# Sliding-window attention and a multiplicative FFN on one core: batch 0's Q and K in thirds, w1 and w2 in column quarters, and a new order of the first phase

## The chip, the core and the metric

The kernel runs on one core of a Trainium2 chip. The metric is the device time of one execution in microseconds (us), median of several runs. Engines are named as in the profile: PE (TensorE, matrix multiplies), PEld (its weight loads), DVE (VectorE), ACT (ScalarE), POOL (GpSimd) and SP (SyncE). Each engine works through its own list of instructions in the order in which the program lists them. POOL also issues the transfers that cast from 32-bit to 16-bit floats on their way into the chip; an instruction that issues a transfer stands in POOL's list like any other.

## What is computed

For 8 batches, 8 heads, 576 tokens and a head width of 64, with q, k and v in 32-bit floats:

```
scores = q @ k.T / 8, kept where 0 <= query - key < 64
attn   = softmax(scores);  x = attn @ v, put together as [4608 tokens, 512]
out    = ((x @ w1) * (x @ w2)) @ w3 @ w_out        w1, w2: [512, 1024]; w3: [1024, 1024]; w_out: [1024, 512]
```

## The kernel before, in words

**Fold.** Since nothing stands between w3 and w_out, the kernel computes `wc = w3 @ w_out` once, in eight blocks of 128 rows. `fold_t(fc)` (line 469) transposes one block of w3 by eight 128-wide multiplies with the identity (line 474) and copies it out of PSUM (476); `fold_mm(fc, c0, c1, cp)` (478) multiplies it with columns c0 to c1 of w_out (481) and copies the result out (482). Four transposed blocks fit at a time.

**Attention.** `load_qk(b, which)` (202) brings Q or K of a batch in by four POOL transfers, one for each pair of heads, into 32 partitions each. In batches 0 to 2 a partition takes runs of 9 tokens (line 200). `transposes(b, which, hh)` (219) turns a half of the heads over on DVE (225). `scores(n)` (272) multiplies for a third of a batch (192 queries, all 8 heads; line 286) into two PSUM tiles `a_ps`; `weigh(d)` (296) takes the exponential of one of these tiles on ACT (303) and cuts the window out, with a multiply by a ready band on DVE (308), or with two or four selects on POOL (258, 260). `values(d)` (314) multiplies with V (337 in the first three batches) and, with the sums of the same multiplication, normalises: a logarithm and an exponential on ACT (343, 344), a multiply on DVE into `xT` (345). There are two `a_ps` buffers in all, for scores and values together. `load_v` (232) brings blocks of 128 tokens of V, `copy_v` (240) copies the overlap of two blocks on DVE; the columns of ones beside V are set once (512). `keep_sums` stores the logarithms for a check at the end.

**FFN.** `ffn_ab(g, fc, nf, lo, hi)` (401) computes `(x @ w1) * (x @ w2)` for a group of 512 tokens or a half of it: matmuls into two of the four `f_ps` buffers (417), a copy of the first on ACT (422), the product on DVE (423). `ffn_o(g, t)` (426) multiplies 128 tokens with `wc` (435), copies (437) and stores through SP (444).

**Order.** The schedule is written out by hand. Lines 516 to 620 are the first phase: the loads of batch 0 and of the weights, the fold, batch 0 and 1 of attention, FFN group 0 and a part of group 1. In it `keep_busy(n)` (502) puts n multiplies of the identity with itself on PE. `make_identity` is two POOL instructions, `make_bands` (265) eight. From `tick(24)` at line 614 on, a loop places attention steps (`tick`) between FFN steps; that loop is the same before and after.

Of the kernel before, what the change touches and what calls it, by code (L numbers as in the profile page):

```python
# [8 lines left out]
FP32 = mybir.dt.float32  # L9
FP16 = mybir.dt.float16  # L10
# [134 lines left out]
def kernel(  # L145
# [22 lines left out]
    NU = 12 * B  # L168
    NS = 3 * B
    SHORT = 3  # L170
    EARLY = 2

    keep = ctx.enter_context(tc.tile_pool(name="keep", bufs=1))
    ident16 = keep.tile([P, P], FP16)
# [22 lines left out]

    t16s, kTs, qTs = {}, {}, {}

    RUN = [9] * 3 + [2] * (B - 3)  # L200

    def load_qk(b, which, *hhs):
        src = k if which == "k" else q
        r = RUN[b]
        if (which, b) not in t16s:
            t16s[which, b] = sb.tile([P, 2, TI * D], FP16, name=which + "16", bufs=2)
        t = t16s[which, b]
        if not hhs:
            for j in range(NJ):
                nc.gpsimd.dma_start(  # L210
                    out=t[32 * j:32 * j + 32].rearrange("p hh (i n) -> p (hh i) n", n=r * D),
                    in_=src[b, 2 * j:2 * j + 2].rearrange("hh (i p r) d -> p (hh i) (r d)", p=32, r=r))
        for hh in hhs:
            for i in range(2):
                nc.gpsimd.dma_start(
                    out=t[:, hh, i * r * D:(i + 1) * r * D],
                    in_=src[b, hh:H:2, i * 32 * r:(i + 1) * 32 * r].rearrange("j (p r) d -> j p (r d)", p=32, r=r))

    def transposes(b, which, hh):

        dst = kTs if which == "k" else qTs
        r = RUN[b]
        if hh == 0:
            dst[b] = sb.tile([P, 2, S, 2], FP16, name=which + "T")
        nc.vector.transpose(  # L225
            dst[b][:, hh].rearrange("q t c -> q (t c)").bitcast(I32).rearrange("q (i p r) -> q i r p", p=32, r=r),
            t16s[which, b][:, hh].bitcast(I32).rearrange("p (i r e) -> p i r e", r=r, e=32))

    def v_heads(b):
        return v16s[b % 2].rearrange("p c j (a e) -> p c (j a) e", a=2)[:, :, :, 0:D]  # L230
# [38 lines left out]

    held = {}  # L270

    def scores(n, now=True):

        b, si = divmod(n, 3)
        kT, qT = kTs[b], qTs[b]
        seg = SEGS[si]
        w = sum(blk[2] for blk in seg)
        s_ps = [ps_a.tile([P, 2, 512], FP32, name="a_ps") for _ in range(2)]
        c0 = 0
        for (k0, q0, m, _) in seg:  # L280
            for a in range(2):
                for c in range(2):
                    for j in range(NJ):
                        part = slice(32 * j, 32 * j + 32)
                        o0 = 256 * a + c0
                        nc.tensor.matmul(s_ps[j // 2][:, j % 2, o0:o0 + m], kT[part, a, k0:k0 + P, c],  # L286
                                         qT[part, a, q0:q0 + m, c], start=(c == 0), stop=(c == 1),
                                         skip_group_check=True)
# [3 lines left out]
        weigh(2 * n)  # L292
        if now:
            weigh(2 * n + 1)

    def weigh(d):

        s_ps = held.pop(d)
        si = d // 2 % 3
        w = s_ps.shape[-1]  # L300

        pt = sb.tile([P, 2, 2, 256], FP16, name="pt", bufs=6)
        nc.scalar.activation(pt[:, :, :, 0:w], s_ps, AF.Exp, bias=-SHIFT, scale=scale)  # L303

        rows = pt.rearrange("k j a n -> k (j a) n")
        if d % 2 == 1 and d < 6 * EARLY:
            band = bands[min(si, 1)]
            nc.vector.tensor_tensor(rows[:, :, 0:w], rows[:, :, 0:w],  # L308
                                    band[:, 0:w].unsqueeze(1).broadcast_to([P, 4, w]), ALU.mult)
        else:  # L310
            select(rows, si)
        probs[d] = pt

    def values(d):
# [4 lines left out]
        pt = probs.pop(d)  # L319
        seg = SEGS[si]  # L320
        q_base = seg[0][1]
        o_ps = ps_a.tile([P, 2, 512], FP32, name="a_ps")
        if jp == 0:
            lns[b, si] = sb.tile([P, NJ, 192], FP32, name="ln_s", bufs=4)
        y = lns[b, si][:, j0:j0 + 2]
        r = sb.tile([P, 2, 192], FP32, name="r")
        x0 = (b * S + q_base) % RING
        xs = xT[:, j0:j0 + 2, x0:x0 + 192]
        if b < SHORT:

            for jj in range(2):
                c0 = 0
                for bi, (k0, q0, n, _) in enumerate(seg):
# [8 lines left out]
            o, total = (o_ps[:, e, 0:384].rearrange("p (j n) -> p j n", j=2) for e in range(2))  # L342
            nc.scalar.activation(y, total, AF.Ln)
            nc.scalar.activation(r, y, AF.Exp, scale=-1.0)  # L344
            nc.vector.tensor_tensor(xs, o, r, ALU.mult)  # L345
            return
        for jj in range(2):
            first = True
            for a in range(2):
                c0 = 0  # L350
                for bi, (k0, q0, n, _) in enumerate(seg):
# [4 lines left out]
                                     start=first, stop=(bi == 1), skip_group_check=True)  # L356
                    first = False
                    c0 += n
        nc.scalar.activation(y[0:D], o_ps[D:P, :, 0:192], AF.Ln)  # L359
        nc.scalar.activation(y[D:P], o_ps[0:D, :, 192:384], AF.Ln)  # L360
        nc.scalar.activation(r, y, AF.Exp, scale=-1.0)  # L361
# [21 lines left out]
    def tick(u):  # L383

        b, r = divmod(u, 12)
        n, m = divmod(u, 4)
        if m == 0 and n < NS:
            scores(n, now=False)
        if m == 1 and n < NS:
            weigh(2 * n + 1)  # L390
        if m in (1, 2) and 6 < n <= NS:
            values(2 * n - 3 + m)
        for e in late.get(r, []):
            event(b, *e)
        if m == 3 and 6 < n <= NS:
            keep_sums(n - 1)
# [54 lines left out]
        return w3a[:, 2 * fc:2 * fc + 2, :] if fc < 4 else \  # L451
            xT[:, fc - 4, 2 * S:2 * S + DF].rearrange("p (a n) -> p a n", a=2)

    def load_w12(i, half):
        cols = slice(half * 512, half * 512 + 512)
        nc.gpsimd.dma_start(out=(w1_sb, w2_sb)[i][:, :, cols],
                            in_=(moe_w1, moe_w2)[i][:, cols].rearrange("(c p) n -> p c n", p=P))

    def load_wo(half):
        cols = slice(half * 256, half * 256 + 256)  # L460
        nc.gpsimd.dma_start(out=wo16[:, :, cols], in_=moe_w_out[:, cols].rearrange("(e p) m -> p e m", p=P))  # L461

    def load_w3(n):
        fc = 2 * n
        dst = w3a[:, 2 * fc:2 * fc + 4, :].rearrange("p (f a) n -> p f (a n)", f=2) if n < 2 else \
            xT[:, fc - 4:fc - 2, 2 * S:2 * S + DF]
        nc.gpsimd.dma_start(out=dst, in_=moe_w3[fc * P:fc * P + 2 * P].rearrange("(f p) n -> p f n", p=P))

    def fold_t(fc):

        w3 = w3_rows(fc).rearrange("p a (e n) -> p (a e) n", n=P)
        tp = ps_f.tile([P, 8, P], FP16, name="f_ps")
        for ec in range(8):
            nc.tensor.transpose(tp[:, ec, :], w3[:, ec, :], ident16)  # L474
# [38 lines left out]

    w3Ts = {}

    load_qk(0, "k")
    make_identity(nc, ident16)
    load_qk(0, "q")
    load_wo(0)
    load_w3(0)  # L520
    make_bands()
    load_w3(1)
    load_wo(1)
    load_w3(2)
    load_v(0, 0, 2, 3)
    for i in range(2):
        ones_of(i, nc.vector)
    for which in "kq":
        for hh in range(2):
            transposes(0, which, hh)  # L530
    keep_busy(120)
    scores(0)
    keep_busy(30)
    fold_t(0)
    fold_t(1)
    scores(1)
    load_w3(3)
    load_v(0, 4, 5)
    fold_mm(0, 0, 256, act_cp)
    fold_mm(1, 0, 256, act_cp)  # L540
    fold_t(2)
    fold_t(3)
    scores(2)
    for i in range(2):
        load_w12(i, 0)
    fold_mm(2, 0, 256, act_cp)
    fold_mm(3, 0, 256, act_cp)
    fold_mm(0, 256, DM, act_cp)
    fold_mm(1, 256, DM, act_cp)
    fold_t(4)  # L550
    fold_t(5)
    fold_mm(2, 256, DM, act_cp)
    fold_mm(3, 256, DM, act_cp)
    copy_v(0, 1)
    fold_mm(4, 0, DM, act_cp)
    values(0)
    values(1)
    fold_t(6)
    fold_mm(5, 0, DM, act_cp)
    values(2)  # L560
    values(3)
    copy_v(0, 4)
    fold_t(7)
    fold_mm(6, 0, DM, act_cp)
    values(4)
    values(5)
    fold_mm(7, 0, DM, act_cp)
    for i in range(2):
        load_w12(i, 1)
    load_qk(1, "k")  # L570
    load_qk(1, "q")
    load_v(1, 0, 2, 3, 4, 5)
    for n in range(3):
        keep_sums(n)
    for fc in range(8):
        ffn_ab(0, fc)
        if 2 <= fc < 6:
            transposes(1, "kkqq"[fc - 2], fc % 2)
    load_qk(2, "k")
    load_qk(2, "q")  # L580
    copy_v(1, 1)
    copy_v(1, 4)
    scores(3)
    ffn_o(0, 0)
    store()
    scores(4)
    load_v(2, 0, 2, 3)
    ffn_o(0, 1)
    store()
    scores(5)  # L590
    transposes(2, "k", 0)
    ffn_o(0, 2, act_cp)
    store()
    values(6)
    transposes(2, "k", 1)
    values(7)
    load_v(2, 4, 5)
    ffn_o(0, 3)
    store()
    values(8)  # L600
    transposes(2, "q", 0)
    values(9)
    load_qk(3, "k")
    load_qk(3, "q")
    ffn_ab(1, 0, 2, 0, 256)
    values(10)
    transposes(2, "q", 1)
    ffn_ab(1, 2, 2, 0, 256)
    values(11)
    for n in range(3, 6):  # L610
        keep_sums(n)
    U0 = 24
    ffn_ab(1, 4, 2, 0, 256)
    tick(24)
# [72 lines left out]
```

## Time and profile before

| | us |
|---|---|
| median of 3 runs (267.65 to 269.23) | 268.73 |
| the profiled execution | 268.59 |
| its span in the trace | 266.8 |
| PE busy in the span | 254.4 (95%) |
| POOL busy | 178.7 (67%) |
| DVE busy | 169.7 (64%) |
| ACT busy | 151.4 (57%) |

What lies around the span is 1.8 us (268.59 - 266.8). The page cuts the span into 40 slices of 6.67 us and gives the busy share of each engine in tenths. The timeline of an engine gives, for each stretch of equal instructions, its start, its length, the line, what it writes and reads, and in square brackets the idle time before it with what ended it. The view by windows adds up each engine's busy time between two moments. The chain that ended last runs over PE for 87% of the span.

### The profile page before, as it was taken

What the parts mean: (1) busy time and instruction counts of PE and PEld (TensorE: products, weight loads), DVE (VectorE), ACT (ScalarE), POOL (GpSimd) and SP (SyncE); (2) the same over time, 40 slices, a digit from 0 to 9 for tenths busy, and PEclk for the clock granted to TensorE, in tenths of its full rate; (3) what the DMA queues carried; (4) which work ended last, traced back from release to release, by engine and by line L of the source; (5) the groups of instructions that cost most, each with busy time, mean ns of one, the idle gap of its engine ahead of it and who ended that gap; (6) DMA issues with size and microseconds to landing.
All of it is one profiled execution on the core that took longest, in us unless ns stands there. A gap on an engine that the chain in (4) does not pass through costs nothing.

```text
span 266.8 us, 6600 instructions
## 1 busy us (share of the span) xinstructions
PE 254.4 (95%) x2608; PEld 149.7 (56%) x2608; DVE 169.7 (64%) x260; ACT 151.4 (57%) x261; POOL 178.7 (67%) x243
## 2 busy tenths in 40 slices
PE   3979999998999999999999999999999999999992
PEld 3968654445886445545556984545455445444441
DVE  6644454978775675986687567668786565564531
ACT  1037474367656577758874855777498748342300
POOL 7979826679879999999898739687766345005000
PEclk9999999999999999999999999999999999999998
DMA  5999999999999999899999765998540040012013
GB/s 81 170 207 186 189 207 201 131 181 138 149 106 62 131 206 77 61 165 162 62 106 180 102 43 64 202 105 57 99 96 4 7 150 6 0 53 108 0 57 109
DMA packets 75380, 29.45 MB, mean 110 GB/s; under 512 B 62369, under 2 KB 69793, under 8 KB 75345
## 3 DMA queue, kind: packets, MB, share of 16 engines
q0 software_dynamic: 69920, 19.41, 74.9%
q1 hardware_dynamic: 5280, 9.46, 10.0%
q8 instruction: 21, 0.34, 0.6%
q14 instruction: 15, 0.11, 0.2%
q10 hardware_dynamic: 144, 0.13, 0.1%
HBM read 38.80 MB, written 9.44 MB: 181 GB/s over the span
## 4 chain that ended last, share of the span: by engine, by line
PE 87%; DMA 4%; POOL 2%; DVE 2%; ACT 2%; issue 1%; POOLq 0%; DVEq 0%
PE f_ps L417 48%; PE f_ps L435 22%; PE a_ps L353 5%; PE a_ps L286 4%; PE f_ps L481 4%; DMA ab<-in_moe_w_dram 4%; PE a_ps L337 3%; ACT pt L303 1%; PE f_ps L474 1%; POOL q L210 1%; POOL k L210 1%; DVE xT L345 1%; DVE kT L225 1%; POOL ab L461 0%; DVE pt L308 0%
## 5 line engine op out<-in xcount | busy, mean ns | idle before, releaser
L417 PE MATMUL f_ps<-xT,w_sb 128*128 128x512 f16 (+1 forms) x704 | 131.5, 341 | 0.0
L417 PEld LDWEIGHTS <-w_sb 128*128 128x128 f16 x704 | 66.3, 98 | 50.7 <-issue 0.2
L423 DVE TENSOR_TENSOR ab<-f_ps,a_sb 128x512 f16<-128x512 f32 x72 | 49.6, 689 | 33.0 <-PE f_ps L417 31.2
L303 ACT ACTIVATE pt<-a_ps 128x1024 f16<-128x1024 f32 (+1 forms) x48 | 44.5, 953 | 45.4 <-PE a_ps L286 45.4
L258 POOL TENSOR_SCALAR_AFFINE_SELECT pt<-pt 128x1024 f16<-128x1024 f16 (+2 forms) x56 | 46.1, 824 | 30.6 <-ACT pt L303 30.5
L435 PE MATMUL f_ps<-wc_sb,ab 128*128 128x512 f16 (+1 forms) x296 | 66.4, 374 | 0.0
L422 ACT COPY a_sb<-f_ps 128x512 f32<-128x512 f32 x72 | 41.8, 581 | 36.9 <-PE f_ps L417 36.4
L260 POOL TENSOR_SCALAR_AFFINE_SELECT pt<-pt 128x1024 f16<-128x1024 f16 (+2 forms) x56 | 46.5, 831 | 3.9
L435 PEld LDWEIGHTS <-ab 128*128 128x128 f16 x296 | 27.3, 98 | 28.8
L238 POOL DMA_DIRECT2D v<-in_v_dram x40 | 34.0, 860 | 1.0 <-issue 0.4
L362 DVE TENSOR_TENSOR xT<-a_ps,r 64x384 f16<-64x384 f32 x30 | 16.5, 550 | 22.0 <-ACT r L361 22.0
L437 DVE COPY t2k<-f_ps 128x512 f32<-128x512 f32 (+1 forms) x35 | 23.7, 679 | 8.4 <-PE f_ps L435 7.9
L210 POOL DMA_DIRECT2D q<-in_q_dram x32 | 19.7, 621 | 11.8 <-DMA w_sb<-in_moe_w_dram 8.3
L210 POOL DMA_DIRECT2D k<-in_k_dram x32 | 20.1, 634 | 1.6 <-POOLq L671 1.0
L353 PEld LDWEIGHTS <-v 128*128 128x128 f16 x240 | 15.1, 98 | 6.4
L345 DVE TENSOR_TENSOR xT<-a_ps,r 128x384 f16<-128x384 f32 x18 | 10.0, 553 | 13.0 <-ACT r L344 13.0
L359 ACT ACTIVATE ln_s<-a_ps 64x384 f32<-64x384 f32 x30 | 14.6, 487 | 5.8 <-PE a_ps L353 5.0
L353 PE MATMUL a_ps<-pt,v 128*128 128x128 f16 x240 | 17.2, 215 | 0.0
L363 DVE TENSOR_TENSOR xT<-a_ps,r 64x384 f16<-64x384 f32 x30 | 16.8, 561 | 0.4
L286 PEld LDWEIGHTS <-kT 32*128 32x128 f16 x768 | 10.9, 92 | 9.6 <-issue 9.3
L361 ACT ACTIVATE r<-ln_s 128x384 f32<-128x384 f32 x30 | 15.7, 523 | 1.0
L225 DVE STREAM_TRANSPOSE qT<-q 128x576 int32<-128x576 int32 x16 | 14.7, 928 | 1.6 <-DMA q<-in_q_dram 1.6
(44 smaller groups left out, 184.9 us busy)
## 6 DMA issues: line engine op xcount, KB each, us to landing
out_dram<-t2k SPq DMA_DIRECT2D x35, 256.0 KB
k<-in_k_dram POOLq DMA_DIRECT2D x32, 144.0 KB, 6.3
q<-in_q_dram POOLq DMA_DIRECT2D x32, 144.0 KB, 5.8
v<-in_v_dram POOLq DMA_DIRECT2D x32, 128.0 KB, 5.0
w_sb<-in_moe_w_dram POOLq DMA_DIRECT2D x4, 512.0 KB, 9.7
ab<-in_moe_w_out_dram POOLq DMA_DIRECT2D x2, 512.0 KB, 9.5
ab<-in_moe_w_dram POOLq DMA_DIRECT2D x2, 512.0 KB, 9.4
xT<-in_moe_w_dram POOLq DMA_DIRECT2D x2, 512.0 KB, 10.4
```

The source lines that it names most:

```text
L210: nc.gpsimd.dma_start(out=t[32 * j:32 * j + 32].rearrange("p hh (i n) -> p (hh i) n", n=r * D), in_=src[b, 2 * j:2 * j + 2].rearrange("hh ...
L238: nc.gpsimd.dma_start(out=vh[lo:P, c], in_=v[b, :, s0:s0 + P - lo, :].rearrange("h s d -> s h d"))
L258: nc.gpsimd.affine_select(out=sl, in_=sl, pattern=pat, compare_op=ALU.is_ge, fill=0.0, base=off, channel_multiplier=-1)
L260: nc.gpsimd.affine_select(out=sl, in_=sl, pattern=[[-s, m] for s, m in pat], compare_op=ALU.is_ge, fill=0.0, base=63 - off, channel_multip ...
L286: nc.tensor.matmul(s_ps[j // 2][:, j % 2, o0:o0 + m], kT[part, a, k0:k0 + P, c], qT[part, a, q0:q0 + m, c], start=(c == 0), stop=(c == 1), ...
L303: nc.scalar.activation(pt[:, :, :, 0:w], s_ps, AF.Exp, bias=-SHIFT, scale=scale)
L353: nc.tensor.matmul(o_ps[:, jj, o0:o0 + n], v16[:, si * 2 + bi, j0 + jj, a * D:a * D + P], pt[:, jj, a, c0:c0 + n], start=first, stop=(bi = ...
L417: nc.tensor.matmul(d[:, f * n + c0:f * n + c1], w[:, dc, (fc + f) * P:(fc + f + 1) * P], xT[:, dc, xc:xc + c1 - c0], start=first, stop=(dc ...
L422: act_cp(a_sb[:, 0:nf * n], a_ps[:, 0:nf * n])
L423: nc.vector.tensor_tensor(ab[:, fc:fc + nf, lo:hi], b_ps[:, 0:nf * n].rearrange("p (f n) -> p f n", f=nf), a_sb[:, 0:nf * n].rearrange("p ...
L435: nc.tensor.matmul(o_ps[:, 0:c1 - c0], ab[:, fc, t * P:t * P + P], wc_sb[:, fc, c0:c1], start=(fc == 0), stop=(fc == 7))
L437: cp(o_sb[:, c0:c1], o_ps[:, 0:c1 - c0])
```

## The change

Three things change in the loads. Q and K of batch 0 come in twelve transfers instead of eight: for each of q and k, each half of the heads (`hh`, the odd or the even ones) and each third of 192 tokens, one transfer into all 128 partitions, in runs of 6 tokens. `transposes` can take one third alone. w1 and w2 come in column quarters of 256 instead of halves of 512, and w3 for blocks 0 and 1 in single blocks. Two functions are cut apart, so that their parts can be placed separately: `weigh` is no longer called by `scores` and takes the engine that cuts the window (DVE or POOL), and `norm` holds what followed the multiplication in `values`. Then the first phase is written out in another order.

```diff
-    RUN = [9] * 3 + [2] * (B - 3)
+    RUN = [6] + [9] * 2 + [2] * (B - 3)
...
+    def third(b, which, hh, i):
+        r = RUN[b]
+        src = k if which == "k" else q
+        return src[b, hh:H:2, i * 32 * r:(i + 1) * 32 * r].rearrange("j (p r) d -> j p (r d)", p=32, r=r)
...
+    def load_third(b, which, hh, i):
+        n = RUN[b] * D
+        nc.gpsimd.dma_start(out=t16_of(b, which)[:, hh, i * n:(i + 1) * n], in_=third(b, which, hh, i))
...
-    def weigh(d):
+    def weigh(d, engine=nc.gpsimd):
...
-        if d % 2 == 1 and d < 6 * EARLY:
+        if engine is nc.vector:
...
-    def load_w12(i, half):
-        cols = slice(half * 512, half * 512 + 512)
+    def load_w12(i, c0, c1):
+        cols = slice(c0, c1)
...
-        dve_cp(w3Ts[fc], tp)
+        cp(w3Ts[fc], tp)
```

The order before stands in lines 516 to 612. The new one, from the first load to the unchanged `U0 = 24`, with several calls on a line:

```
load_third(0,'k',1,0); load_w3(2,2); load_w3(0,1); make_identity(nc, ident16); ones_of(1, nc.vector); make_bands()
load_w3(1,1); load_wo(0,256); transposes(0,'k',1,0); keep_busy(115); load_third(0,'q',1,0); fold_t(1, dve_cp)
load_third(0,'k',0,0); fold_t(2, act_cp); load_third(0,'q',0,0); transposes(0,'k',0,0); load_wo(256,512)
fold_t(0, act_cp); load_third(0,'k',0,1); keep_busy(20); ones_of(0, nc.gpsimd); load_third(0,'q',1,1); load_w3(4,2)
load_third(0,'k',1,1); fold_t(3, dve_cp); transposes(0,'q',0,0); load_third(0,'q',0,1); transposes(0,'q',1,0)
transposes(0,'q',1,1); load_v(0,2); load_v(0,0); load_w3(6,2); load_w12(0,256,512); keep_busy(20)
fold_mm(0,0,256, act_cp); load_third(0,'k',0,2); fold_mm(2,0,256, act_cp); scores(0); weigh(0, nc.vector)
fold_mm(3,0,256, dve_cp); transposes(0,'k',0,1); load_v(0,3); weigh(1, nc.vector); fold_mm(0,256,DM, act_cp)
fold_mm(1,256,DM, act_cp); load_third(0,'q',0,2); fold_mm(1,0,256, act_cp); fold_mm(2,256,DM, act_cp)
load_third(0,'k',1,2); transposes(0,'k',1,1); load_w12(1,0,256); fold_t(4, dve_cp); transposes(0,'q',0,1)
fold_t(5, dve_cp); fold_mm(4,0,DM, dve_cp); load_third(0,'q',1,2); scores(1); copy_v(0,1); weigh(2, nc.vector)
fold_mm(3,256,DM, dve_cp); load_w12(0,0,256); fold_mm(5,0,256, dve_cp); weigh(3, nc.gpsimd); values(0); norm(0)
values(1); fold_t(7, dve_cp); load_v(0,5); norm(1); fold_mm(5,256,DM, act_cp); load_v(0,4); transposes(0,'q',0,2)
transposes(0,'k',0,2); load_w12(0,512,768); transposes(0,'k',1,2); transposes(0,'q',1,2); fold_t(6, act_cp)
load_w12(1,256,512); values(2); norm(2); load_w12(1,512,768); values(3); norm(3); load_qk(1,'k')
fold_mm(7,0,DM, dve_cp); fold_mm(6,0,DM, dve_cp); scores(2); keep_sums(0); copy_v(0,4); load_qk(1,'q')
weigh(4, nc.vector); ffn_ab(0,0,2,0,256); load_w12(0,768,1024); load_w12(1,768,1024); values(4)
weigh(5, nc.vector); norm(4); ffn_ab(0,2,2,0,256); values(5); norm(5); load_qk(2,'k'); load_qk(2,'q'); load_v(1,2)
ffn_ab(0,4,2,0,256); transposes(1,'k',0); load_v(1,0); load_v(2,0); load_v(1,3); transposes(1,'k',1)
transposes(1,'q',0); ffn_ab(0,4,2,256,512); ffn_ab(0,0,2,256,512); transposes(1,'q',1); ffn_ab(0,2,2,256,512)
ffn_ab(0,7); ffn_ab(0,6); scores(3); load_v(1,4); transposes(2,'k',0); load_v(1,5); transposes(2,'k',1)
weigh(6, nc.vector); weigh(7, nc.gpsimd); ffn_o(0,0, dve_cp); copy_v(1,1); load_v(2,4); scores(4); load_v(2,5)
weigh(8, nc.gpsimd); weigh(9, nc.vector); ffn_o(0,1, dve_cp); store(); scores(5); weigh(10, nc.gpsimd)
weigh(11, nc.vector); ffn_o(0,2, dve_cp); values(6); values(7); norm(6); norm(7); store(); load_qk(3,'k')
load_v(2,3); keep_sums(1); load_v(2,2); load_qk(3,'q'); ffn_o(0,3, act_cp); keep_sums(2); transposes(2,'q',1)
copy_v(1,4); store(); values(8); values(9); norm(8); keep_sums(3); norm(9); transposes(2,'q',0)
ffn_ab(1,0,2,0,256); values(11); values(10); norm(10); norm(11); keep_sums(4); keep_sums(5); ffn_ab(1,2,2,0,256)
```

More of the change, by code (lines that the diff above doesn't have):

```diff
@@ L534 @@
[L534 to L547, printed above, removed]
+    load_w3(1, 1)
+    load_wo(0, 256)
+    transposes(0, 'k', 1, 0)
+    keep_busy(115)
+    load_third(0, 'q', 1, 0)
+    fold_t(1, dve_cp)
+    load_third(0, 'k', 0, 0)
+    fold_t(2, act_cp)
+    load_third(0, 'q', 0, 0)
@@ L556 @@
+    transposes(0, 'k', 1, 1)
+    load_w12(1, 0, 256)
+    fold_t(4, dve_cp)
+    transposes(0, 'q', 0, 1)
+    fold_t(5, dve_cp)
+    fold_mm(4, 0, DM, dve_cp)
+    load_third(0, 'q', 1, 2)
+    scores(1)
+    copy_v(0, 1)
+    weigh(2, nc.vector)
+    fold_mm(3, 256, DM, dve_cp)
+    load_w12(0, 0, 256)
+    fold_mm(5, 0, 256, dve_cp)
+    weigh(3, nc.gpsimd)
     values(0)
+    norm(0)
     values(1)
-    fold_t(6)
-    fold_mm(5, 0, DM, act_cp)
+    fold_t(7, dve_cp)
+    load_v(0, 5)
+    norm(1)
@@ L560 @@
+    fold_mm(5, 256, DM, act_cp)
+    load_v(0, 4)
+    transposes(0, 'q', 0, 2)
+    transposes(0, 'k', 0, 2)
+    load_w12(0, 512, 768)
+    transposes(0, 'k', 1, 2)
+    transposes(0, 'q', 1, 2)
+    fold_t(6, act_cp)
+    load_w12(1, 256, 512)
     values(2)
+    norm(2)
+    load_w12(1, 512, 768)
     values(3)
-    copy_v(0, 4)
-    fold_t(7)
-    fold_mm(6, 0, DM, act_cp)
+    norm(3)
+    load_qk(1, 'k')
+    fold_mm(7, 0, DM, dve_cp)
+    fold_mm(6, 0, DM, dve_cp)
+    scores(2)
+    keep_sums(0)
@@ L565 @@
+    copy_v(0, 4)
+    load_qk(1, 'q')
+    weigh(4, nc.vector)
+    ffn_ab(0, 0, 2, 0, 256)
+    load_w12(0, 768, 1024)
+    load_w12(1, 768, 1024)
     values(4)
+    weigh(5, nc.vector)
+    norm(4)
+    ffn_ab(0, 2, 2, 0, 256)
     values(5)
[L567 to L578, printed above, removed]
@@ L597 @@
-    load_v(2, 4, 5)
-    ffn_o(0, 3)
+    weigh(10, nc.gpsimd)
+    weigh(11, nc.vector)
+    ffn_o(0, 2, dve_cp)
+    values(6)
+    values(7)
+    norm(6)
+    norm(7)
+    store()
+    load_qk(3, 'k')
+    load_v(2, 3)
+    keep_sums(1)
+    load_v(2, 2)
+    load_qk(3, 'q')
+    ffn_o(0, 3, act_cp)
+    keep_sums(2)
+    transposes(2, 'q', 1)
+    copy_v(1, 4)
     store()
     values(8)
-    transposes(2, "q", 0)
     values(9)
-    load_qk(3, "k")
-    load_qk(3, "q")
+    norm(8)
+    keep_sums(3)
@@ L605 @@
+    norm(9)
+    transposes(2, 'q', 0)
     ffn_ab(1, 0, 2, 0, 256)
+    values(11)
     values(10)
-    transposes(2, "q", 1)
+    norm(10)
+    norm(11)
+    keep_sums(4)
+    keep_sums(5)
     ffn_ab(1, 2, 2, 0, 256)
-    values(11)
-    for n in range(3, 6):
-        keep_sums(n)
     U0 = 24
```

180 lines of the change are left out of this document (107 added, 73 removed).

## The prediction, made before the changed kernel ran

> **What bounds the kernel now.** I read the page first. PE is busy for 95% of the span, and from the third of the 40 slices on hardly ever below nine tenths:
>
> ```profile
> PE 254.4 (95%) x2608; PEld 149.7 (56%) x2608; DVE 169.7 (64%) x260; ACT 151.4 (57%) x261; POOL 178.7 (67%) x243
> ...
> PE   3979999998999999999999999999999999999992
> ...
> DMA  5999999999999999899999765998540040012013
> ```
>
> The transfers are as dense as PE up to slice 22, so a load that comes later than now has little room. The change touches only what lies ahead of `tick(24)`, whose first matmul (line 286) stands at 72.87 us in PE's timeline. The view by windows, cut there and at the borders of the stages (start, length, PE's busy time, ...), shows how much PE could gain:
>
> ```profile
> 13.50:17.43 3.93, 2.51 (x64) 2.14 (x63) 1.51 (x2) 1.51 (x2) 3.86 (x5) 1.00 1.14 212
> 17.43:39.94 22.51, 22.14 (x321) 16.29 (x322) 10.16 (x19) 13.84 (x27) 14.53 (x21) 1.00 1.45 194
> 39.94:53.96 14.02, 14.02 (x65) 6.13 (x64) 9.49 (x12) 5.27 (x9) 8.93 (x14) 1.00 2.03 167
> 53.96:72.87 18.91, 17.95 (x273) 11.40 (x273) 14.88 (x22) 13.29 (x22) 16.76 (x22) 1.00 1.14 154
> 72.87:100.00 27.13, 27.13 (x362) 17.15 (x362) 18.22 (x28) 17.11 (x28) 24.80 (x35) 1.00 1.13 127
> ```
>
> PE is idle for 1.42 + 0.37 + 0 + 0.96 = 2.75 us between 13.5 and 72.87, and not at all afterwards: what the first phase gains or loses arrives at the end undiminished. PE's timeline tells where the idle time and the filler stand:
>
> ```profile
> 4.57 9.02 PE L506 MATMUL f_ps<-ident 128*128 128x128 f16 x120 [4.57 <-POOL ident masks.py:199]
> 13.52 0.29 PE L286 MATMUL a_ps<-qT,kT 32*128 32x128 f16 x8
> 14.51 0.41 PE L286 MATMUL a_ps<-qT,kT 32*128 32x128 f16 x24 [0.70 <-DVE qT L225]
> 14.85 1.85 PE L506 MATMUL f_ps<-ident 128*128 128x128 f16 x30
> 17.43 1.07 PE L474 MATMUL f_ps<-ident,ab 128*128 128x128 f16 x16 [0.73 <-DMA ab<-in_moe_w_dram]
> ...
> 39.94 14.09 PE L417 MATMUL f_ps<-xT,w_sb 128*128 128x512 f16 x64
> ```
>
> PE starts at 4.57, when the identity is there; 150 filler multiplies (line 506) bridge the wait for Q, K and w3.
>
> **PE's own work, by the change.** (a) Start: ahead of the identity POOL issues three loads instead of four. Four took 2.44 us; a third counts 0.61, a two-block w3 0.72, a single block I put between the two kinds at 0.6. PE starts 0.5 us earlier (bounds 0 and 0.8: nothing ahead but less than one issue saved, or one whole issue and the 0.2 gap). (b) Filler: 115 + 20 + 20 instead of 150, at 1.85/30 = 62 ns: +0.3. (c) Six of the eight `ffn_ab(0, ..)` become halves with two blocks. Such a group takes 1.85 us (66.18 to 68.03 later in the trace), one of line 417 above 14.02/8 = 1.75: six times 0.1 = +0.6. `fold_mm(5)` in halves: under 0.05. (d) The idle 2.75 us go where other work is ready. The floor is -0.5 + 0.3 + 0.6 - 2.75 = -2.35 us.
>
> **What the new order has to meet.** I walk PE through the new list with those durations (a `fold_t` 0.48, a half `fold_mm` 0.875, scores 0.6, values 0.5). The first filler ends at 12.7; fold, scores 0 to 2 and values 0 to 3 end at 37.0; group 0 of the FFN ends at 52.9, where scores(3) start (53.96 now); tick(24) is reached at 71.0 (now 72.87). Does each operand come in time? For the loads, POOL's timeline holds a rule of this program:
>
> ```profile
> 27.30 3.07 POOL L456 DMA_DIRECT2D w_sb<-in_moe_w_dram x4
> 30.34 1.12 POOL L210 DMA_DIRECT2D k<-in_k_dram x2
> 31.76 1.09 POOL L210 DMA_DIRECT2D k<-in_k_dram x2 [0.29 <-DMA v<-in_v_dram]
> 34.67 0.55 POOL L210 DMA_DIRECT2D q<-in_q_dram x1 [1.82 <-DMA w_sb<-in_moe_w_dram]
> 37.18 0.55 POOL L210 DMA_DIRECT2D q<-in_q_dram x1 [1.97 <-DMA w_sb<-in_moe_w_dram]
> 39.72 0.55 POOL L210 DMA_DIRECT2D q<-in_q_dram x1 [2.00 <-DMA w_sb<-in_moe_w_dram]
> 42.77 0.55 POOL L210 DMA_DIRECT2D q<-in_q_dram x1 [2.51 <-DMA w_sb<-in_moe_w_dram]
> ```
>
> The four w pieces land 7.1, 8.8, 10.6 and 12.9 us after their issues, at 34.4, 36.9, 39.4 and 42.5, and each time one q issue goes on 0.3 us later: an issue waits for the landing of the load eight before it. Smaller pieces therefore mean fewer bytes under way, and POOL's selects queue behind such a wait.
>
> Pace: a 512 KB piece of w3, w1 or w2 takes 2.55 us (landings 14.7, 17.4, 19.9, 22.5), that of w_out too, though its rows are as short as those of the new w quarters; so a quarter counts 1.3 and the quarters lose nothing. V takes 0.93 a block, K and Q of batch 1 0.75 a piece (43.1 to 48.6). A third of 96 KB does not occur before. Low bound 0.48, at w3's bytes per us; the queue's 18112 packets of the first 60 us took 137.3% of 16 engines, 73 ns each, so 128 of them take 0.58; high bound 1.0, the pace of the larger pieces of batch 0's Q (landings 9.0 to 12.0). I take 0.5, as they fill all partitions like w3.
>
> POOL issues 4 thirds, 4 w quarters and one w3 piece more (4 x 0.57 + 4 x 0.77 + 0.5 = 5.9 us), sets one V's ones (128x3072; its 128x128 and 128x256 memsets took 0.23 and 0.33, so 2.7 by their slope; bounds 2.6, DVE's memset, and 4.0, twelve of 0.33), and cuts four windows instead of six (2 x 2.4 off): +3.8 us, all ahead of their need. The landings that result, and when PE or DVE wants them: w3 block 1 10.9 (12.7), w_out 12.6 and 16.7 (16.9, 20.1), w3 blocks 4, 5 20.3 (23.6), 6, 7 25.8 (30), last thirds 31.5 (33). At `weigh(3)` POOL waits for the exponential of scores(1) and selects until 31.6, with nine loads behind it; the queue runs dry at 32.9 and restarts at 34.4 (a V block issued at 60.63 into an empty queue landed 3.7 later, 2.8 beyond its 0.93). Then w2's second quarter 38.7 (39.3), K of batch 1 43.0 (44.2), Q 46.0 (46.6), the last w quarters 47.3 and 48.6 (49.5, 50.3). All hold, the tightest by 0.6.
>
> DVE: `transposes(1, ..)` take 1.21 each and three stand in a row behind the product of `ffn_ab(0,4)`; from 44.2 to 47.8 no product is made, the next one frees its PSUM buffer at 48.5, and PE wants it at 48.1: +0.4. A third's transposition is put at 0.42 (1.21/3; at most 0.77, the shortest of a whole one) with over 1 us of room each. The copy of `fold_t(4)` before `fold_mm(4)` costs 0.05 to 0.2. Sum: -2.35 + 0.45 = -1.9 us. ACT's extra fold copies (about 1.0 each by the 0.95 of line 303) lie under PE's filler and folds; uncovered they would cost 1 us each.
>
> Against the profiled execution's own 268.59 (0.14 below the median) that is **266.7 us**.
>
> **Rivals.** *The gain is given back behind the first phase.* `load_v(2,2)` now stands behind four K loads of batch 3, is issued at about 67.6 and lands near 73 (V blocks there took 3.7 to 6.0, K pieces 0.8 each); DVE's `copy_v(2,1)` waits for it with all products of group 1 behind it. PE has 0.6 us of room. With 6.0 and packets at the 1.5 us that a K piece's would take alone, 2.4 us are lost; with half of the spread 1.0: 267.7, no change that can be told. For it: three queues are near full there; against: PSUM holds two products.
>
> *The loads come late (the slower side).* If a third takes 1.0 us, twelve cost 6.0 more; 1.55 are absorbed where the queue runs dry, 0.6 by Q's margin, and DVE then waits in `transposes(1,'q',0)`, in order, with the products behind it: 3.9 us, net +2.0, **270.6**. It decides from 0.84 us per third on (break-even), from 0.95 beyond the 0.5% that a measurement of this kernel can tell from no change. For it: batch 0's Q did take 1.0 a piece; against: in four times 32 partitions, and batch 1's took 0.75.
>
> *Thirds on a quarter of the engines.* A third's 128 packets as 32 on each of four of the 16 DMA engines: 32 x 73 ns = 2.3 us. If engines waited for each other at each wide transfer, the seven groups of thirds would take 16.4 instead of 6 us, 10.4 later, 8.2 after the two margins: **274.9**. If they run on by themselves and thirds fall on different engines, it is 0.58 a third and nothing is lost. No row before shows a transfer of such a shape.
>
> The Trainium skill speaks for this shape: "DMA: Bandwidth & Descriptors", section "Why a DMA increments its semaphore by 16 and not by 1", says that a transfer is split along the slowest dimension of each side over the largest number up to 16 that divides both, and the source of a third has four heads there. By the same section the next such transfer takes the next engines, so the sum by that page is again 266.7; by fixed engines it would be 274.9.
>
> *It does not do what it says.* If idle time were no bound, PE's list alone would grow by 0.4 and the end would not move earlier: 269.0. The zero idle time after 72.87 speaks against it.
>
> **Chances.** Forecast 0.45; given back or list alone 0.27; late loads 0.24; a quarter of the engines 0.04. Faster by over 0.5% 0.45, within 0.27, slower 0.28. The range reaches from the floor with the earliest start (268.59 - 2.65 = 265.9) to the late loads (270.6, and 0.2 for the copy of fold_t(4)): 265.9 to 270.8; the forecast's own is 265.9 to 267.3.
>
> **What would show it.** PE's first filler starts at 4.1; no PE idle over 0.5 us before tick(24); line 286 for scores(3) at 52.9, for tick(24) at 71.0; thirds landing about 0.5 us apart where they follow each other; POOL idle at 27 to 29 before the select of `weigh(3)`; three transposes in a row on DVE from 44. Thirds 2 us behind their neighbours, PE idle behind DVE at 46 to 50, or behind `copy_v` at 73, would prove the forecast wrong.

## The result, and the profile after

The changed kernel takes **271.67 us** (median of four runs, 271.13 to 272.82), the kernel before 268.71 on the same chip: a ratio of 1.0124, 95% interval [1.0099, 1.0150]. The forecast was 266.7, 1.9 us faster; it is 3.0 us slower, outside the range. The profiled execution took 272.82 and is the slowest of the four; its span is 271.0. Some executions of a kernel run in a slower state at a lower clock; medians and ratios here and below leave them out.

The page of the changed kernel, the lines that answer to those shown of before, and the casting queue's line of the third part:

```profile
PE 255.1 (94%) x2669; PEld 155.4 (57%) x2669; DVE 168.6 (62%) x272; ACT 151.8 (56%) x259; POOL 184.1 (68%) x247
...
PE   3997999799978999999999999999999999999993
...
DMA  5999999999999799799969991995760021013013
...
q0 software_dynamic: 77232, 19.42, 75.7%
```

PE is busy for 0.7 us longer than before (254.4), near the forecast's +0.9 (filler and halves), but four slices show gaps where there were none: the fourth (20 to 27 us), the eighth and the twelfth at 7, the thirteenth at 8. The DMA row is at 9 from the second slice to the thirteenth, as before, and shows nothing of the loss: it is a share of time, not of bytes. What differs is the queue's count of packets, 77232 for the same bytes, 69920 before.

PE's timeline of the changed kernel (start, length, line, operation; in brackets the idle time before it and what ended it); line 292 is line 286 of before:

```profile
19.54 0.76 PE L292 MATMUL a_ps<-qT,kT 32*128 32x128 f16 x32 [0.58 <-DVE qT L231]
...
27.50 1.90 PE L495 MATMUL f_ps<-ab,w3T 128*128 128x512 f16 x8 [1.84 <-DVE w3T L490]
...
54.30 2.76 PE L432 MATMUL f_ps<-xT,w_sb 128*128 128x512 f16 x12 [1.59 <-DMA w_sb<-in_moe_w_dram]
57.00 0.53 PE L292 MATMUL a_ps<-qT,kT 32*128 32x128 f16 x32
...
74.61 0.53 PE L292 MATMUL a_ps<-qT,kT 32*128 32x128 f16 x32
...
82.36 1.03 PE L432 MATMUL f_ps<-xT,w_sb 128*128 128x256 f16 x8 [2.76 <-DVE ab L438]
```

Four waits make 6.8 us, where 2.75 were to vanish. The two moments that the prediction named are late: scores(3) at 57.0 (before 53.96, forecast 52.9), `tick(24)` at 74.6 (72.87, forecast 71.0). DVE's timeline tells what stands behind three of the waits:

```profile
18.03 0.53 DVE L231 STREAM_TRANSPOSE kT<-k 128x192 int32<-128x192 int32 x1 [3.66 <-DMA k<-in_k_dram]
...
26.41 0.52 DVE L231 STREAM_TRANSPOSE kT<-k 128x192 int32<-128x192 int32 x1 [2.50 <-DMA k<-in_k_dram]
26.78 0.67 DVE L490 COPY w3T<-f_ps 128x1024 f16<-128x1024 f16 x1
...
80.92 0.35 DVE L250 COPY v<-v 64x512 f16<-64x512 f16 x1 [5.13 <-DMA v<-in_v_dram]
```

Twice DVE stands still for a third of K. The copy that PE wants at 27.5 had its input ready and stood behind the second of them. At 80.92 it is the copy of V's block 2 of batch 2 that waits, with all products of `ffn_ab(1, ..)` behind it.

A later run of the same kernel unchanged (below: *again*) gave 271.89, with PE waits of 0.84, 1.61, 0.34 and 3.65 at about the same places: all come again, but the one at 54 falls from 1.59 to 0.34 and the last grows by 0.9. A single wait of one execution is thus known to about 1 us; the sum is 6.4 in place of 6.8.

### The profile page after: what moved, and what is told of

Its sections match the earlier page's. It is cut to its first block, busy times and chain, and to the rows that moved or that the text cites. A ratio compares the mean times of both kernels' runs of the same rounds, so it can differ in the third digit from the quotient of the medians.

```text
span 271.0 us, 6723 instructions
## 1 busy us (share of the span) xinstructions
PE 255.1 (94%) x2669; PEld 155.4 (57%) x2669; DVE 168.6 (62%) x272; ACT 151.8 (56%) x259; POOL 184.1 (68%) x247
## 3 DMA queue, kind: packets, MB, share of 16 engines
q0 software_dynamic: 77232, 19.42, 75.7%
## 4 chain that ended last, share of the span: by engine, by line
PE 72%; DMA 14%; POOL 9%; issue 1%; DVE 1%; ACT 1%; DVEq 0%; POOLq 0%
PE f_ps L432 39%; PE f_ps L450 22%; DMA k<-in_k_dram 6%; PE a_ps L346 5%; DMA v<-in_v_dram 4%; PE a_ps L292 4%; DMA w_sb<-in_moe_w_dram 3%; POOL v L244 1%; PE a_ps L334 1%; POOL w_sb L471 1%; POOL v L526 1%; POOL k L222 1%; POOL k L206 1%; POOL q L222 1%; ACT pt L306 1%
## 5 line engine op out<-in xcount | busy, mean ns | idle before, releaser
L432 PEld LDWEIGHTS <-w_sb 128*128 128x128 f16 x752 | 70.8, 98 | 50.7 <-issue 2.9
L450 PE MATMUL f_ps<-wc_sb,ab 128*128 128x512 f16 (+1 forms) x296 | 66.4, 374 | 0.0
L264 POOL TENSOR_SCALAR_AFFINE_SELECT pt<-pt 128x1024 f16<-128x1024 f16 (+2 forms) x53 | 43.7, 825 | 30.5 <-ACT pt L306 30.5
L266 POOL TENSOR_SCALAR_AFFINE_SELECT pt<-pt 128x1024 f16<-128x1024 f16 (+2 forms) x53 | 43.8, 826 | 3.6
L206 POOL DMA_DIRECT2D q<-in_q_dram x28 | 17.9, 646 | 6.4 <-DMA w_sb<-in_moe_w_dram 5.3
L231 DVE STREAM_TRANSPOSE kT<-k 128x576 int32<-128x576 int32 (+1 forms) x20 | 15.3, 782 | 8.5 <-DMA k<-in_k_dram 8.5
L206 POOL DMA_DIRECT2D k<-in_k_dram x28 | 17.7, 642 | 0.3 <-DVE v L248 0.2
L231 DVE STREAM_TRANSPOSE qT<-q 128x576 int32<-128x576 int32 (+1 forms) x20 | 15.4, 777 | 3.3 <-DMA q<-in_q_dram 3.3
L495 PE MATMUL f_ps<-ab,w3T 128*128 128x256 f16 (+1 forms) x104 | 14.9, 298 | 1.8 <-DVE w3T L490 1.8
```

Source lines behind the costliest of these rows:

```text
L206: nc.gpsimd.dma_start(out=t[32 * j:32 * j + 32].rearrange("p hh (i n) -> p (hh i) n", n=r * D), in_=src[b, 2 * j:2 * j + 2].rearrange("hh ...
L231: nc.vector.transpose(dst[b][:, hh].rearrange("q t c -> q (t c)").bitcast(I32).rearrange("q (i p r) -> q i r p", p=32, r=r)[:, part], t16s ...
L264: nc.gpsimd.affine_select(out=sl, in_=sl, pattern=pat, compare_op=ALU.is_ge, fill=0.0, base=off, channel_multiplier=-1)
L266: nc.gpsimd.affine_select(out=sl, in_=sl, pattern=[[-s, m] for s, m in pat], compare_op=ALU.is_ge, fill=0.0, base=63 - off, channel_multip ...
L432: nc.tensor.matmul(d[:, f * n + c0:f * n + c1], w[:, dc, (fc + f) * P:(fc + f + 1) * P], xT[:, dc, xc:xc + c1 - c0], start=first, stop=(dc ...
L450: nc.tensor.matmul(o_ps[:, 0:c1 - c0], ab[:, fc, t * P:t * P + P], wc_sb[:, fc, c0:c1], start=(fc == 0), stop=(fc == 7))
```

## The experiments

Each run stands beside runs of the kernel before on its own chip (medians 268.37 to 268.63); all ratios are to these, with 95% intervals. Runs of different chips are better compared by their ratios than by their medians.

| run | what it changes | median us | ratio |
|---|---|---|---|
| again | the changed kernel | 271.89 | 1.0116 [1.0085, 1.0147] |
| wide | thirds read 128 rows | 269.20 | 1.0014 [0.9986, 1.0043] |
| V first | V blocks 2, 3 of batch 2 ahead of K of batch 3 | 269.94 | 1.0057 [1.0022, 1.0091] |
| weigh(3) on DVE | the window of `weigh(3)` | 270.97 | 1.0100 [1.0054, 1.0146] |
| wide + V first | both | 268.09 | 0.9977 [0.9949, 1.0005] |
| V first + weigh(3) | narrow thirds, as in the change | 269.43 | 1.0020 [0.9996, 1.0044] |
| all three | wide, V first, weigh(3) on DVE | 266.44 | 0.9936 [0.9916, 0.9957] |
| narrow alone | before, with Q and K of batch 0 of that shape | 271.85 | 1.0142 [1.0117, 1.0167] |
| quarters alone | before, with w1, w2 in quarters | 268.58 | 0.9992 [0.9968, 1.0017] |
| first third, then rest | only the first thirds narrow | 278.96 | 1.0354 [1.0316, 1.0392] |
| the same, reordered | Q's rest behind a transposition | 270.39 | 1.0068 [1.0041, 1.0095] |
| one transposition moved | before, DVE's order only | 267.51 | 0.9952 [0.9931, 0.9974] |

**The shape of a third, and the place of V.** The theory: a third whose source has four heads as its slowest dimension runs on 4 of the 16 DMA engines. *Wide* keeps bytes, run length, order and destination, and gives the source 128 rows as its slowest dimension:

```diff
-        return src[b, hh:H:2, i * 32 * r:(i + 1) * 32 * r].rearrange("j (p r) d -> j p (r d)", p=32, r=r)
+        c = (3 * hh + i) * r * D
+        return src[b].rearrange("h (x n) d -> (h x) (n d)", x=16)[:, c:c + r * D]
```

> The changed kernel, but each third reads 128 rows of 6 tokens at one even distance over all heads, instead of 32 rows in each of four heads: the same bytes, packets and number of issues, other tokens, so attention of batch 0 is computed from the wrong Q and K. Theory A (a third runs on 4 of the 16 DMA engines and the transfers behind it are held up): the software queue's packets fall by 12 x 384 = 4608 to 72,624; w_out's halves land 3 us earlier than the 16.1 and 21.0 of now; the PE idle times of 1.84 at 27.5 and 1.59 at 54.3 go; scores(3) start at 53.5 instead of 57.0 and the time falls by about 3.3 to 268.4, the wait for V of batch 2 staying. Rival B (more and smaller transfers, each issue waiting for the landing of the eighth before it, and longer issues on POOL): landings move by less than 1 us and the time by less than 0.7, 271.0 to 271.7.

*V first* moves two calls:

```diff
-    load_qk(3, 'k')
     load_v(2, 3)
-    keep_sums(1)
     load_v(2, 2)
+    load_qk(3, 'k')
+    keep_sums(1)
```

> The changed kernel with one move: the loads of V blocks 3 and 2 of batch 2 stand ahead of K of batch 3 instead of behind it. Theory (two separate losses: late loads before scores(3), and copy_v(2,1) held by V block 2 of batch 2): the 5.1 us wait on DVE at 75.8 and the 2.8 us of idle PE at 79.6 go, nothing else moves: 268.9 against 271.7. Rival (the wait at 80 us is only the late end of one and the same lateness of the transfers): K and Q of batch 3 are late in its place, at most 1 us is won, 270.7 or more.

Then both together, and the third suspect alone, the selects of `weigh(3)` with nine loads behind them:

> Both edits before together (attention of batch 0 from the wrong tokens again). Theory A with two separate losses: about 266, near the 266.7 of the forecast, PE without idle times over 0.5 us between 13 and 90 us. Rival B: 268.2 to 268.9, the move of V alone.

```diff
-    weigh(3, nc.gpsimd)
+    weigh(3, nc.vector)
```

> The changed kernel with the window of weigh(3) cut on DVE instead of POOL, so that the nine loads behind it no longer wait for the exponential of scores(1). By the rule of eight in flight the first of them may go at 32.0 instead of 34.2, but the fifth waits for the last third of K at 36.3 anyway, against 37.4 now: the loads win about 1 us, the idle 1.59 us of PE at 54.3 shrink to 0.6, the time falls to 270.7. If POOL's select is what makes the loads late (the rival to the four engines for that stage), they win the full 2.2 us and the time falls to 269.5.

*Wide* took 2.5 us off (269.20 against 271.67; 3.3 expected), and the queue's packets fell to 72624: 4608 fewer, 384 for each of the twelve thirds. All of them are packets of 4 bytes: the trace of the changed kernel has 6576 of these, that of *wide* 1968, which is 16 for each of its 123 transfers. The first third landed 3.0 us after its issue, 4.9 in the changed kernel.

The trace doesn't name the engine of a packet, but at the first third the packets tell it. Its 128 packets of 768 B run from 3.07 to 5.97 us; a wide third's, in *all three*, run from 2.89 to 4.02. Towards the end the narrow third's stand in four trains, with a packet every 60 ns in each, and after the last packet of each train comes one of 4 bytes (at 5.55, 5.77, 5.84 and 5.95). So 32 packets pass on each of four engines, 32 x 60 ns = 1.9 us at the least. The other 396 small packets would be 33 for each of the twelve engines left, padding without data; they are done by 3.45.

The windows view of half microseconds in which hardly anything else is under way (start:end, length, busy PE, PEld, DVE, ACT, POOL, clock, DMA share, GB/s), first of the changed kernel, then of *all three*, whose thirds are wide:

```profile
3.00:3.50 0.50, 0.00 (x0) 0.00 (x0) 0.50 (x1) 0.00 (x0) 0.50 (x2) 1.00 0.75 21
3.50:4.00 0.50, 0.00 (x0) 0.00 (x0) 0.50 (x1) 0.00 (x0) 0.42 (x3) 1.00 0.35 29
4.00:4.50 0.50, 0.17 (x2) 0.17 (x3) 0.23 (x1) 0.00 (x0) 0.50 (x2) 1.00 0.82 66
```

```profile
3.00:3.50 0.50, 0.00 (x0) 0.00 (x0) 0.50 (x1) 0.00 (x0) 0.50 (x2) 1.00 0.65 78
3.50:4.00 0.50, 0.00 (x0) 0.00 (x0) 0.50 (x1) 0.00 (x0) 0.42 (x2) 1.00 1.53 134
4.00:4.50 0.50, 0.37 (x4) 0.37 (x5) 0.34 (x2) 0.00 (x0) 0.43 (x3) 1.00 0.29 20
```

The DMA moves 21 and 29 GB/s with the narrow third where it moves 78 and 134 with the wide one, which is done at 4. (From 3.5 on the first packets of w3 are among them, 8 in the wide case and 3 in the narrow one.)

What missed: w_out was expected 3 us earlier with wide thirds and came 0.7 and 1.0 earlier (15.3 and 19.9, against 16.1 and 20.9). POOL issues no load while it builds identity and bands (3.5 to 6.7 us), the rate falls to 78 GB/s between 8.5 and 9 us in *all three* too, and the one w3 block issued next lands 5.3 us later; that delay is there with wide thirds as well. The wait at 27.5 shrank from 1.84 to 0.83 and did not go.

*V first* took 1.7 off (2.8 expected). The wait at 82 goes, but PE waits for 1.88 at 67.57, behind DVE. There a copy of V for batch 1 had waited 1.88 for its load (1.43 in the changed kernel), and the multiply behind it took 2.44 us where the same one took 0.69 in the changed kernel; what slowed it the trace doesn't tell. Waits at this place also stand in *again* (0.46) and *wide* (0.94), so it is not shown that the move makes one. *weigh(3) on DVE* alone took 0.7 off (1.0 expected), and its interval overlaps that of the change: by itself it tells nothing.

*Wide + V first* was expected at about 266 and gave 268.09: what each took off alone (2.5 + 1.7) is 0.6 more than what both took off. PE still waits for 1.14 us at 52.7, behind a transposition of Q on DVE, and for 0.98 at 66.4, behind a select on POOL.

**All three, and its counterpart with narrow thirds.**

> The changed kernel with wide thirds (wrong tokens in batch 0, as above), V of batch 2 ahead of K of batch 3, and the window of weigh(3) cut on DVE. If the loads behind weigh(3) are what still keeps that kernel 1.4 us above the forecast, w1, w2, K and Q of batch 1 come 1 to 2 us earlier, scores(3) start at 53 to 53.5 and the time is 266.6 to 267.2. If the transfers themselves are the limit there, it stays within 0.5 of 268.1.

> The changed kernel with its thirds as they are, V of batch 2 ahead of K of batch 3 and the window of weigh(3) on DVE: the kernel of 266.4 us but for the shape of the thirds, and computing the reference. If the shape of the thirds costs the same 3 us whatever stands behind it, 269.2 to 269.5; if the two repairs leave enough room to hide late thirds, 267 or less.

PE's timeline of *all three*:

```profile
18.74 0.53 PE L293 MATMUL a_ps<-qT,kT 32*128 32x128 f16 x32
...
24.06 1.07 PE L489 MATMUL f_ps<-ident,xT 128*128 128x128 f16 x16 [0.33 <-DMA xT<-in_moe_w_dram]
...
49.16 4.49 PE L433 MATMUL f_ps<-xT,w_sb 128*128 128x256 f16 x24 [0.23 <-DVE ab L439]
53.58 0.53 PE L293 MATMUL a_ps<-qT,kT 32*128 32x128 f16 x32
...
71.17 0.53 PE L293 MATMUL a_ps<-qT,kT 32*128 32x128 f16 x32
```

With the three obstacles away the kernel takes 266.44, 0.3 from the forecast; `tick(24)` stands at 71.17 where the prediction put 71.0. (It reads other tokens for batch 0, so it is a measurement of the order, not a kernel to use.) The narrow counterpart takes 269.43 and shows PE waits of 1.11, 1.54, 0.68 and 0.86 us again: **the shape alone costs 3.0 us** by the medians, 2.3 by the ratios (1.0020 and 0.9936). It costs about as much with the other obstacles left in: 2.5 by the medians in the changed kernel, 1.8 with V moved alone (269.94 and 268.09). So 2 to 3 us is what the runs give. Taken away one at a time, the three obstacles are worth 2.5, 1.7 and 0.7 us, 4.9 in sum; taken away together, 5.2 (271.67 and 266.44). The landings show where the shape acts: w_out's first half lands at 16.7 with narrow thirds and at 15.4 with wide ones, the last third at 37.2 and 34.2, a delay of 2.9 us that has grown over twelve thirds.

POOL's timeline of the changed kernel shows what `weigh(3)` does to the loads:

```profile
32.02 1.10 POOL L264 TENSOR_SCALAR_AFFINE_SELECT pt<-pt 128x1024 f16<-128x1024 f16 x1 [0.70 <-ACT pt L306]
33.19 1.10 POOL L266 TENSOR_SCALAR_AFFINE_SELECT pt<-pt 128x1024 f16<-128x1024 f16 x1
34.24 1.62 POOL L244 DMA_DIRECT2D v<-in_v_dram x2
```

From 31.3 to 34.2 no load is issued. Taking that away from *wide + V first* gives 266.44 after 268.09, 1.65 us by the medians and 1.1 by the ratios; the two intervals overlap ([0.9949, 1.0005] and [0.9916, 0.9957]), so its size is less sure than the other two.

**The shape and the quarters by themselves, in the kernel before.** `load_qk` of before has a branch, unused there, that loads one half of the heads and half of the tokens into 128 partitions, again with four heads as the slowest dimension:

```diff
-    load_qk(0, "k")
+    load_qk(0, "k", 0, 1)
...
-    load_qk(0, "q")
+    load_qk(0, "q", 0, 1)
```

> The kernel before with one edit: Q and K of batch 0 come as halves of the heads and of the tokens into all 128 partitions, eight transfers of the same bytes as now, but from 32 rows in each of four heads, like the thirds. Theory A (four engines each, the next transfer on the next four): 8 x 384 = 3072 packets more, 72,992; a transfer takes 32 x 0.12 = 3.9 us instead of 1.0, but four go side by side; the first lands 2 us later than 3.4 after its issue, the last about where it does now; the time stays within 0.7 of 268.5. If all narrow transfers fell on the same four engines, the last of Q would land 30 us after the first issue and the time would be over 285.

I expected the eight transfers to overlap, each on its own four engines, and to cost next to nothing. They cost 3.4 us (271.85 against 268.49). Issued 0.74 us apart (2.96 us for four), K's four landed at 7.7, 9.3, 11.0 and 12.2, some 1.5 apart, and the queue has 3072 packets more, again 384 each. They do overlap: over all eight the landings are 1.1 us apart (7.7 to 15.6), hardly more than the 1.0 of the wide ones before (4.8 to 12.1). But the first comes 2.8 us later than before, and the rest never make that up: the last comes 3.5 later. DVE's timeline, first of before, then of that run:

```profile
8.34 2.27 DVE L225 STREAM_TRANSPOSE kT<-k 128x576 int32<-128x576 int32 x2 [0.90 <-DMA k<-in_k_dram]
```

```profile
9.41 1.23 DVE L225 STREAM_TRANSPOSE kT<-k 128x576 int32<-128x576 int32 x1 [1.97 <-DMA k<-in_k_dram]
12.27 1.22 DVE L225 STREAM_TRANSPOSE kT<-k 128x576 int32<-128x576 int32 x1 [1.63 <-DMA k<-in_k_dram]
```

Before, both halves of K were turned over from 8.34 to 10.6 without a wait between them. PE's second part of scores(0) starts at 16.94 instead of 14.51 behind a wait of 1.69, and scores(3) at 57.24 instead of 53.96.

The quarters alone:

```diff
-        cols = slice(half * 512, half * 512 + 512)
+        cols = slice(quarter * 256, quarter * 256 + 256)
```

> The kernel before with w1 and w2 in column quarters at their places, eight issues instead of four. Theory (bytes count, not pieces): same pace as w_out's halves with equally short rows, POOL pays 4 x 0.77 = 3.1 us of issues under cover: 268.5 within 0.6. Rival (each issue waits for the eighth before it, so eight quarters keep half the bytes under way): the second half of w1 and w2 lands over 1 us later than 42.5, PE waits for it at the fifth step of FFN group 0, 269.5 or more.

268.58 beside 268.49: they cost nothing that can be measured.

**Wide loads with the right tokens.** A source of 32 rows of whole runs is wide again. Only the first thirds stay narrow; tokens 192 to 575 come in four transfers per tensor into 32 partitions each, on top of *V first* and *weigh(3) on DVE*:

```diff
+            nc.gpsimd.dma_start(
+                out=t[32 * j:32 * j + 32][:, :, 6 * D:TI * D],
+                in_=src[0, 2 * j:2 * j + 2, 192:S].rearrange("hh (p r) d -> p hh (r d)", p=32, r=12))
```

> The kernel of the run before this one, but only the first third of Q and K of batch 0 comes in four narrow transfers; the other 384 tokens come in runs of 12, by one transfer for each pair of heads into 32 partitions (both halves of the heads at once), eight wide transfers of 96 KB, as many in all. It computes the reference. Theory A (narrow transfers are what costs): eight of twelve are gone, two thirds of the 3 us come back, 267.3, below the kernel before. Rival: the last third now comes 2 us ahead of its need and holds up w3 and V, PE waits for blocks 4 to 7 of w3, 268.5 or more.

It missed by 11.7 us. DVE's timeline and the windows of that run:

```profile
28.03 0.52 DVE L245 STREAM_TRANSPOSE qT<-q 128x192 int32<-128x192 int32 x1 [8.07 <-DMA q<-in_q_dram]
```

```profile
20.00:25.00 5.00, 0.30 (x8) 0.15 (x8) 0.00 (x0) 0.00 (x0) 4.86 (x8) 0.93 1.08 173
25.00:30.00 5.00, 1.40 (x29) 1.06 (x29) 0.52 (x1) 0.76 (x2) 3.90 (x6) 0.50 1.58 179
30.00:35.00 5.00, 5.00 (x27) 3.63 (x26) 2.87 (x5) 1.50 (x4) 3.26 (x6) 0.54 1.54 191
```

The transposition of the odd heads' first third waited for the load of Q's rest, which stands ahead of it in the program and writes other columns of the same tile. PE was idle for 8.3 us (20.3 to 28.6), and its granted clock (third column from the right) fell to 0.50 and 0.54 until 35 us. With the load placed behind that transposition:

```diff
-    load_rest('q')
     fold_t(3, dve_cp)
     transposes(0, 'q', 0, 0)
     transposes(0, 'q', 1, 0)
+    load_rest('q')
```

> As x8 (V block 2 of batch 2 ahead of K of batch 3, weigh(3) on DVE, only the first third of batch 0's Q and K narrow, tokens 192 to 575 in four loads of 32 partitions for each of Q and K), except that the four loads of Q's rest stand behind the transpositions of Q's first third in the program. In x8 the transposition of the odd heads' first third waited 8.07 us for those loads, though it reads other columns, and PE was idle for 8.29 us with its clock at about half until 35. Theory: the wait was the whole loss. The 8.29 us go, and about 10 us at half clock cost 5 us less: 278.96 - 8.3 - 4 to 5 = 266 to 267.5, that is the 266.4 of x5 plus up to 1 us for the four narrow first thirds (about 0.98 to 0.995 of the kernel before: 0.99 to 0.996). Rival: the narrow first thirds hold up w_out and the fold as in the changed kernel, and the rest comes late too: 268.5 to 269.5, as x9; then PE stays idle by over 1 us between 18 and 30, waiting for a transposition of Q or K.

The long wait is gone (8.6 us less), so it was the loss of the run before; but 270.39 is the rival's side, and a little beyond it: no better than twelve narrow thirds (269.43). PE waits for 0.49 us before scores(0), which starts at 19.84 (18.74 in *all three*), and for 1.23 us at 26.30, for w3 and not for a transposition as the rival had it; scores(3) starts at 55.81. Four narrow first thirds, and Q's rest held to 20.4, are enough to lose what the rest wins. How the loss is shared between the two this run doesn't tell.

**A version that beats both.** In before, PE's wait of 0.78 us at 65 stands behind DVE. One transposition goes behind `values(7)`:

```diff
-    transposes(2, "k", 1)
     ...
+    transposes(2, "k", 1)
```

> The kernel before with one move: the second transposition of K of batch 2 stands behind values(7) instead of between values(6) and values(7), so that values(9) no longer wait 0.78 us for a normalisation behind it on DVE. If that wait is real lost time, 0.7 us less, 267.8; if the transposition then delays the next normalisation or the copy of ffn_o(0,3), no change, 268.5.

267.51, ratio 0.9952 [0.9931, 0.9974]: faster than both kernels by little, but clear of the noise; `tick(24)` stands at 72.13 (72.87). The wait in before, then in this run:

```profile
65.61 0.64 PE L337 MATMUL a_ps<-pt,v 128*64 128x128 f16 x16 [0.78 <-DVE xT L345]
```

```profile
64.42 1.08 PE L337 MATMUL a_ps<-pt,v 128*64 128x128 f16 x32 [0.29 <-DVE xT L345]
```

The unchanged kernel a second time, beside these:

> The changed kernel once more, beside the others: 271.7 within 1 us. If the idle times of PE (1.84 at 27.5, 1.59 at 54.3, 2.76 at 82.4) belong to the order, all three come again; if they were this execution's bad luck with the transfers, they move by over 1 us.

## Why the prediction was wrong

**The step that failed** is the pace of the loads: "A third of 96 KB does not occur before. ... I take 0.5, as they fill all partitions like w3." The number of partitions was the wrong row to go by. A third ran on four DMA engines, 1.9 us at the least and 2.9 for the first one, and the shape cost the kernel 2 to 3 us (269.43 against 266.44, both with V moved and `weigh(3)` on DVE), and 3.4 in the kernel before. In the terms of the walk, it put the last third back by 2.9 us, 0.24 for each of the twelve. The way from late loads to lost time was right: counted like the late-loads rival, where all that goes beyond margins of 2.15 us is lost, the landings of the last third (31.5 in the walk, 34.24 wide, 37.15 narrow) give 267.3 and 270.2; measured were 266.44 and 269.43. The mechanism of the four engines was on the list, with a chance of 0.04 and with the clause that it loses nothing "if they run on by themselves and thirds fall on different engines". The chance was too small. The clause was half right: in *narrow alone* the transfers do run side by side, 1.1 us apart in the mean, but the first lands 2.8 us later than a wide one, and that is lost. The two bounds, 0.48 and 1.0, were both taken from transfers on all 16 engines (before has 1824 packets of 4 bytes, 16 for each of its 114 loads through POOL, so none is padded), and did not hold the case.

The rule that I cited spoke of this. The Trainium skill, "DMA: Bandwidth & Descriptors", section "Why a DMA increments its semaphore by 16 and not by 1", splits a transfer over the largest number up to 16 that divides the slowest dimension of both sides; the trace agrees: four heads, four trains of packets. I let its second half, the next transfer on the next engines, take the cost away; no run here bears that out as a price of nothing.

**V behind K of batch 3** was a rival, priced at 1.0 with 2.4 as its end. The block was issued with its neighbour at 71.9 and DVE's copy ran at 80.92; PE lost 2.76 in the trace, and moving V won 1.7. The place and the mechanism were right, the size was near the far end. The wait is smaller where the loads ahead of it come earlier: 1.86 in *wide*, 1.29 in *weigh(3) on DVE*, against 2.76 and 3.65 in the two runs of the changed kernel.

**`weigh(3)`** was held harmless: the walk let the queue run dry at 32.9 and restart at 34.4 and found all loads in time. The selects ended at 34.2 instead of 31.6, and the last two w quarters landed at 51.3 and 54.3, not 47.3 and 48.6. Worth 1.1 to 1.65 us once the other two are gone, 0.7 in the changed kernel; in both cases the intervals overlap.

**The early loads** were mis-sized even without the narrow shape: w_out at 15.3 and 19.9 with wide thirds, against 12.6 and 16.7 in the walk, with no load issued while POOL builds the bands; in *all three* the last third lands at 34.2, against 31.5. A third's issue takes POOL 0.67 to 0.73 us, not 0.57.

**What held.** PE's own sum (-1.9): 266.44 and `tick(24)` at 71.17 in the run without the three obstacles, against 266.7 and 71.0. That they meet so closely is in part luck: scores(3) stands at 53.58, 0.7 later than forecast, the stretch from there to `tick(24)` takes 17.6 us where the forecast had 18.1, and the last third lands 1.2 us after the time (33) at which I had it wanted without PE waiting for it. PE starts at 4.13 there and at 4.33 in the changed kernel (before 4.57, forecast 4.1). The idle time does go where other work is ready: 0.9 us are left of 2.75. The quarters lose nothing. An issue does wait for the load eight before it: the change's 13th load goes out 0.3 us after the landing of the fifth (16.34 and 16.05), the 17th 0.3 after that of the ninth (21.22 and 20.94). The jam of three transposes on DVE costs 0.23 in *all three*, 0.4 forecast.

**Open** stays whether the four engines or the 384 padding packets of each third cost more. At the first third it is the engines: the padding is done by 3.45, the data at 5.97. In the full queue no run separates them: with narrow thirds all 4-byte packets of the trace take 40.8 us more than with wide ones, 2.6 us for each of 16 engines, which is of the size of the delay. A narrow third's issue also costs POOL some 0.14 us more, 1.7 for twelve. Nor was it tried whether a layout of Q and K exists that reads wide, fills 128 partitions and keeps the right tokens.

## What to carry to other kernels

Price a new transfer by the slowest dimension of its source and of its destination, not by its bytes or partitions alone: here four heads there meant four DMA engines, and the number of packets in the queue's line gave it away. When a profile shows each engine almost full, a list of rivals is not enough: ask what happens if several come true together. Here three did, and their losses nearly added up (4.9 us one at a time, 5.2 together). A load behind a select on the issuing engine, or behind four others, is a wait of its own, and a load that writes a part of a tile can hold up a reader of another part.

## What the runs showed of the hardware

- A transfer whose packets run in four trains brings 384 four-byte packets more than a wide one, exactly, in the queue's count of each run (12 x 384 = 4608 between *wide* and the change, 8 x 384 = 3072 in *narrow alone*). That is 32 for each of the twelve engines without data, though the trace doesn't name the engine of a packet.
- In the run with 8.3 us in which PE did nothing (20.3 to 28.6) its granted clock was halved from 24.3 to 34.6 us, from 4.0 us after the start of the idle stretch to 6.0 after its end. The Trainium skill, "TensorE: Matmul & The Clock Gate", section "Part 1: The HAM clock gate (the "warmup" mystery)", says that an idle stretch of some 3.4 us halves the clock; this trace agrees.
- The issue of a narrow third costs POOL more: 0.67 to 0.73 us, against 0.53 to 0.59 us for a wide one of the same bytes (the first of each 0.93 and 0.79).
